# A fused attention and state-space kernel: x loaded in other runs, half of its transposes copied as 32-bit pairs, the first query projected into a score bank

## The chip, the cores and the metric

The kernel runs on one core of a Trainium2 chip. The metric is device time in microseconds (us) of one execution, the median of several. A profiled execution gives a trace; its span runs from the first to the last instruction, and a little time lies around it. The engines are TensorE (PE, its weight loads PEld), VectorE (DVE), ScalarE (ACT), GpSimd (POOL) and SyncE (SP, which issues most of the transfers).

## The reference, cut to what matters

Two branches read the same x (2048 tokens of 448 bfloat16 numbers) and are mixed by a gate:

```python
x = A_x
g = _sigmoid((x * gate_w).sum(-1, keepdims=True))
a = _A_ref(x, A_wq, A_wk, A_wv, A_wo)
b = _B_ref(x, B_A_re, B_A_im, B_B_re, B_B_im, B_C_re, B_C_im, B_log_dt, B_Dskip)
return g * a + (1 - g) * b
```

Branch A is attention with 16 query heads of 28 and one shared key and value head:

```python
q = (x @ wq).reshape(B, S, H, Dh).transpose(0, 2, 1, 3)
k = x @ wk
v = x @ wv
scores = jnp.einsum("bhqd,bkd->bhqk", q, k) * (Dh ** -0.5)
p = _softmax(scores, axis=-1)
o = jnp.einsum("bhqk,bkd->bhqd", p, v)
return o.transpose(0, 2, 1, 3).reshape(B, S, H * Dh) @ wo
```

Branch B is a long convolution of each channel of x with a kernel K that is built from 256 complex modes: K is the real part of the sum over n of C * exp(dt * A * l) * dt * B, for l from 0 to 2047.

## The kernel before, in words

**The long part.** The 16 x 16 x 4 score tiles (128 keys x 512 queries each) go through ACT's exponential at L1428 in sets of three and two tiles in turn. The scores come from TensorE into the five banks 0 to 4 of PSUM (`psS`), tile t in bank t % 5; bank 6 (`psB`) gathers the product with v; banks 5 and 7 are a pool of two that all other work borrows one after the other (`grp()`, with `lock` and `unlock`). Sets 0 to 5 take the query from `qT` (L1373), later ones from `qM` (L1396), a spread copy of `qT` that four transfers of POOL's queue make (L915). Beside the exponentials, VectorE builds tables for K, and TensorE makes K and the convolution.

**The start**, which the change touches. `loads` issues the transfers on SP's queue in the order x0, x1, x2, `raw0` (A_im, for branch B), x3, wq, wv with gate_w, `raw1` (A_re) and further ones; log_dt and wk go by ACT's queue. A block q of x is 512 tokens: partition p gets tokens 4p to 4p+3 of it, one run of 3584 bytes. `prep_x` then does, for q = 0 to 3:

- 16 transposes on TensorE (L668), eight for each half hp, into banks 2 * (q % 2) + hp;
- a copy of each half (112 x 1024) out of PSUM, which also puts the tokens, that lie 4 apart, in order: by VectorE (L680) for hp 1 of blocks 0, 1, 2, by ACT (L678) for the other five;
- the k projection (L688) into bank 4 (block 3: a bank of the pool) and its eviction by ACT to `kT` (L701); block q + 1 must wait for that of block q;
- `km`, the largest |k|, on VectorE (L696), and the v projection (L709).

From the four `km` VectorE makes `Wb` (L718, L720, L723): a matrix that gives each query its own bound, to be subtracted in the scores. The last step is `self.wbl`. The first query (`qproj(0)`): four matmuls with Wq (L893) into a bank of the pool, their absolute values on VectorE (L899), a matmul with `Wb` on top (L902), and the copy to `qT` (L905), for which the first scores wait. Wq is the wq transfer, spread by a copy of VectorE (L581).

At the same time `prep_params` starts branch B. `raw0`, transposed (L817), becomes a phase on VectorE (L828, L831, L832) and two sines on ACT (L834, L835). `raw1`, transposed, becomes t0 on VectorE (L828 again, through the helper `vt`, made at L839), from which ACT makes six exponentials: L840, and five of L843. A load of ACT's table stands between sines and exponentials. At L854 a further operation of VectorE is held back until `wbl` by an entry in `pg.after`.

**What sets the order.** Nothing runs in the order of the source. `Prog.schedule` plans all operations ahead with assumed times (the number that each `pg.op` is given, a model for transfers, fixed delays from engine to engine) and writes each engine's queue. At each step it takes, over all engines, the operation with the smallest (start, `pr`, index): what can start first goes first, and `pr` decides only among operations that could start at the same time, a lower one first. `pg.after[i] = j` keeps i from being planned before j. The chip then runs each queue in that order, whatever the real times are.

Of the kernel before, what the change touches and what calls it, by code (L numbers as in the profile page):

```python
# [7 lines left out]
ALU = mybir.AluOpType  # L8
AF = mybir.ActivationFunctionType
AX = mybir.AxisListType  # L10
BF = mybir.dt.bfloat16
F32 = mybir.dt.float32
P = 128

S = 2048
D = 448
# [3 lines left out]
DT = 112  # L20
# [20 lines left out]
XQ = NT * 512  # L41
QS = 4 * D + 64
GATE = (30, 35)
XDVE = ((1, 0), (1, 1), (1, 2))
WARM = 64
HELD = ((27, 3), (27, 9), (27, 15), (27, 21))
ROWS = 400
# [37 lines left out]
def dram(t, off, dims):  # L85
    return bass.AP(tensor=t.tensor, offset=t.offset + off, ap=[list(d) for d in dims])
# [326 lines left out]
def el(n, rate=0.96, fix=68):  # L413
    return fix + n / rate
# [14 lines left out]
class Kernel:  # L429
# [117 lines left out]
    def loads(self):  # L547
        pg, ins = self.pg, self.ins
# [1 line left out]
        x = ins["A_x"]  # L550

        def lx(q):
            pg.dma([(self.xst.v(0, P, q * QS, [[1, 4 * D]]), dram(x, q * 4 * P * D, [[4 * D, P], [1, 4 * D]]))],
                   (128, 3584), f"x{q}", wr=[("xst", q)], fac=0.85)
        self.raw = self.T
        self.late = []
        raw = self.raw
# [95 lines left out]
    def prep_x(self):  # L653
        pg = self.pg
        xst, kT = self.xst, self.kT
        sm = self.small
        for i in range(18):
            pg.op("pe", lambda e: e.matmul(self.psS.v(0, P, 4 * 512, [[1, 256]]), self.cst.v(0, P, 512, [[1, P]]), self.cst.v(0, P, 512, [[1, 256]]),
                                           start=True, stop=True, tile_position=(0, 0)), 213, rd=[("cst", 1)], wr=["warm", ("b", 4)], pr=3)
        for q in range(4):  # L660
            for hp in range(2):
                b = 2 * (q % 2) + hp
                t, o = self.bank(b, True)

                def mm(e, q=q, hp=hp, t=t, o=o):
                    for Tl in range(2):
                        for k in range(4):
                            r = e.matmul(t.v(0, P, o + 512 * Tl + 128 * k, [[1, 128]]),  # L668
                                         xst.v(0, P, q * QS + k * D + 2 * hp + Tl, [[4, P]]),
                                         self.ident.v(0, P, 0, [[1, P]]), is_transpose=True, tile_position=(0, 0))  # L670
                    return r
                pg.op("pe", mm, 600, rd=[("xst", q), "xpad", "id"], wr=[("b", b)])
                xT, xo = self.xq(q)
                dst = xT.v(0, DT, xo + 2 * hp * 512, [[512, 2], [4, 128], [1, 4]])
                src = t.v(0, DT, o, [[512, 2], [1, 128], [128, 4]])
                key = ("xT", hp, q)
                if (hp, q) not in XDVE:
                    pg.op("act", lambda e, d=dst, s=src: e.activation(d, s, AF.Copy), 1000, rd=[("b", b)], wr=[key])  # L678
                else:
                    pg.op("dve", lambda e, d=dst, s=src: e.tensor_copy(d, s), 1130, rd=[("b", b)], wr=[key])  # L680
            G = self.grp() if q == 3 else None
            t, o = self.bank(4)
            pk = (lambda G=G: G.v(0, P, 0, [[1, 512]])) if q == 3 else (lambda t=t, o=o: t.v(0, P, o, [[1, 512]]))
            bk = ("kx", 3) if q == 3 else ("b", 4)

            def mk(e, q=q, pk=pk, xT=xT, xo=xo):
                for T in range(NT):
                    r = e.matmul(pk(), self.Wk.v(0, DT, T * P, [[1, P]]),  # L688
                                 xT.v(0, DT, xo + T * 512, [[1, 512]]),
                                 start=(T == 0), stop=(T == 3), tile_position=(0, 0))  # L690
                return r
            o = pg.op("pe", mk, 1100, rd=["Wk"] + self.xk(q), wr=[bk], lock=G)
# [3 lines left out]
            km = lambda q=q, src=src: pg.op("dve", lambda e: e.tensor_reduce(  # L696
                sm.v(0, P, 8 + q, [[1, 1]]), src(), AX.X, ALU.max, apply_absolute_value=True), 600,
                rd=[bk if q == 3 else ("kT", q)], wr=[("km", q)])
            if q == 3:
                km()  # L700
            pg.op("act", lambda e, kv=kv, pk=pk: e.activation(kv, pk(), AF.Identity, bias=sm.v(0, P, 0, [[1, 1]])), 600,  # L701
                  rd=[bk, "s0"] + ([("km", 3)] if q == 3 else []), wr=[("kT", q)], pr=-2, unlock=G)
            if q < 3:
                km()

            for kt in range(4 * q, 4 * q + 4):
                def mv(e, kt=kt, xT=xT, xo=xo):
                    for T in range(NT):
                        r = e.matmul(self.psB.v(0, P, 32 * kt, [[1, 29]]), xT.v(0, DT, xo + T * 512 + 128 * (kt % 4), [[1, 128]]),  # L709
                                     self.Wv.v(0, DT, T * 32, [[1, 29]]), start=(T == 0), stop=(T == 3), tile_position=(0, 0))  # L710
                    return r
                pg.op("pe", mv, 140, rd=["Wv", "Wvg"] + self.xk(q), wr=[("b", 6)], pr=0.5)
            if q:
                o = pg.dma([(dram(self.XS, (q - 1) * DT * XQ, [[XQ, DT], [1, XQ]]), xT.v(0, DT, xo, [[1, XQ]]))],
                       (112, 4096), f"xs{q}", rd=self.xk(q), wr=[("XS", q)], pr=0.15)
                for i in self.late:
                    pg.after[i] = o.i
# [67 lines left out]
    def prep_params(self):  # L785
# [50 lines left out]
        pg.op("act", lambda e: e.activation(self.small.v(0, P, 3, [[1, 1]]), self.small.v(0, P, 2, [[1, 1]]), AF.Exp), 1340,  # L836
              rd=["dum", K(2), K(3)], wr=["dum2"], pr=-0.9)
        p1, k1 = trans(1, 1)
        vt(tt(0), p1, dtb, ALU.mult, [k1, "dt"], [K(0)], 1, unlock=p1)  # L839
        pg.op("act", lambda e: e.activation(t(5), t(0), AF.Exp), 950, rd=[K(0)], wr=[K(5)], pr=-1)  # L840
        for lv in range(5):
            ap9 = self.mq.v(0, P, lv * W2, [[32, 2], [64, NC], [1, 32]])
# [40 lines left out]
    def qproj(self, i):  # L883
        pg = self.pg
        qc, g = i // 4, i % 4
        s = i % 2
        X = ("qx", i)
        G = self.grp()
        px = lambda: G.v(0, P, 0, [[1, 512]])

        pr = 0.2 if i == 0 else 1.45 if i < 4 else 1.5
        for T in range(NT):
            pg.op("pe", lambda e, T=T: e.matmul(  # L893
                px(), self.Wq.v(0, DT, T * 512 + g * 128, [[1, 128]]),
                self.xT.v(0, DT, T * 512, [[1, 512]]), start=(T == 0), stop=(T == 3),
                tile_position=(0, 0), skip_group_check=True), 226,
                rd=["Wq"] + self.xk(0) + (["kap"] if i == 1 else []), wr=[X, ("q", s)], pr=pr, lock=G if T == 0 else None)
        av = self.qT.v(0, P, 512 * s, [[1, 512]])
        pg.op("dve", lambda e: e.tensor_reduce(  # L899
            av, G.v(0, P, 0, [[1, 512], [1, 1]]), AX.X, ALU.max, apply_absolute_value=True), el(512),  # L900
            rd=[X], wr=[("q", s)], pr=pr)
# [3 lines left out]
        o = pg.op("dve", lambda e: e.tensor_copy(self.qT.v(0, P, 512 * s, [[1, 512]]), px()), el(512),  # L905
                  rd=[X], wr=[("q", s)], pr=pr, unlock=G)
        if i == 0:
            self.qc0 = o.i
        if i in (3, 7, 11):
# [639 lines left out]
```

## Time and profile before

| | us |
|---|---|
| Median of three runs (497.34 to 498.5) | 497.38 |
| The profiled execution | 497.66 |
| Its span | 495.9 |
| PE busy | 461.8 |
| VectorE busy | 458.3 |
| ACT busy | 483.8 |
| POOL busy | 183.7 |
| First copy of x on ACT starts (L678) | 7.14 |
| First exponential of the scores starts (L1428) | 21.39 |

The granted clock of TensorE is 1.0 throughout. In the profile a line of the timeline gives the start, the duration, the engine, the line of the kernel, the operation, what it writes and reads with shapes, and in brackets how long its engine had been idle and what ended that. A line with "x2" is two such operations, whose durations are merged. A duration of VectorE or ACT overlaps the next one's start a little; where work is added up, the step from one start to the next is the better measure.

### The profile page before, as it was taken

What the parts mean: (1) busy time and instruction counts of PE and PEld (TensorE: products, weight loads), DVE (VectorE), ACT (ScalarE), POOL (GpSimd) and SP (SyncE); (2) the same over time, 40 slices, a digit from 0 to 9 for tenths busy, and PEclk for the clock granted to TensorE, in tenths of its full rate; (3) what the DMA queues carried; (4) which work ended last, traced back from release to release, by engine and by line L of the source; (5) the groups of instructions that cost most, each with busy time, mean ns of one, the idle gap of its engine ahead of it and who ended that gap; (6) DMA issues with size and microseconds to landing.
All of it is one profiled execution on the core that took longest, in us unless ns stands there. A gap on an engine that the chain in (4) does not pass through costs nothing.

```text
span 495.9 us, 17277 instructions
## 1 busy us (share of the span) xinstructions
PE 461.8 (93%) x7559; PEld 208.2 (42%) x7645; DVE 458.3 (92%) x872; ACT 483.8 (98%) x436; POOL 183.7 (37%) x331
## 2 busy tenths in 40 slices
PE   8899999999999999989989999999999999999997
PEld 6432233353443444444334344444534344444544
DVE  6999999999999999999999999999999999995324
ACT  6999999999999999999999999999999999999995
POOL 2102034234242528247707452643843525142110
PEclk9999999999999999999999999999999999999999
DMA  8997694927618554866943962698494685976752
GB/s 234 333 222 164 125 155 108 269 89 227 176 33 283 158 164 127 252 201 138 290 108 68 273 191 65 197 232 228 121 292 124 189 272 134 265 216 223 217 176 71
DMA packets 110055, 91.86 MB, mean 185 GB/s; under 512 B 35386, under 2 KB 105068, under 8 KB 109980
## 3 DMA queue, kind: packets, MB, share of 16 engines
q1 hardware_dynamic: 99322, 78.91, 57.9%
q0 software_dynamic: 10384, 11.70, 9.9%
q8 instruction: 60, 0.98, 0.8%
q10 hardware_dynamic: 274, 0.14, 0.1%
q14 instruction: 15, 0.12, 0.1%
HBM read 73.61 MB, written 5.23 MB: 159 GB/s over the span
## 4 chain that ended last, share of the span: by engine, by line
ACT 87%; PE 5%; DMA 2%; SPq 0%; issue 0%
ACT expT L1428 87%; DMA T<-KP_scratch 2%; PE psS L1373 1%; PE psS L1396 1%; PE psB L1349 1%; PE psB L1449 0%; PE psS L1286 0%; SPq L164 0%; PE psS L1047 0%; PE psS L893 0%; PE psB L1355 0%; PE psX L1047 0%; PE psS L776 0%; PE psX L1114 0%; PE psX L1135 0%
## 5 line engine op out<-in xcount | busy, mean ns | idle before, releaser
L1428 ACT ACTIVATE expT<-psS 128x1536 bf16<-128x1536 f32 (+1 forms) x410 | 464.2, 1407 | 1.1 <-PE psS L1396 0.4
L988 DVE TENSOR_TENSOR tab<-tab,mbf 128x512 bf16<-128x512 bf16 (+4 forms) x140 | 139.3, 998 | 0.0
L1373 PE MATMUL psS<-qT,kT 29*128 29x512 bf16 x684 | 95.7, 385 | 12.2 <-ACT expT L1428 7.1
L1449 PE MATMUL psB<-expT,vaug 128*32 128x512 bf16 x1000 | 99.9, 390 | 0.3
L1396 PE MATMUL psS<-qM,kT 128*128 128x512 bf16 x240 | 78.0, 382 | 13.1 <-issue 8.3
L164 POOL DMA_DIRECT2D KP_scratch<-kstg x104 | 57.3, 558 | 65.6 <-DVE kstg L1059 60.0
L1003 DVE TENSOR_TENSOR tab<-tab 128x256 bf16<-128x256 bf16 (+4 forms) x140 | 77.0, 570 | 0.0
L1449 PEld LDWEIGHTS psB<-expT,vaug 128*32 128x32 bf16 x1000 | 25.6, 93 | 72.6 <-issue 70.7
L164 POOL DMA_DIRECT2D qM<-qT x64 | 32.7, 518 | 58.1 <-DVE qT L905 37.5
L164 POOL DMA_DIRECT2D U<-T x49 | 36.7, 753 | 37.7 <-DMA U<-T 16.3
L1373 PEld LDWEIGHTS psS<-qT,kT 29*128 29x128 bf16 x684 | 23.7, 91 | 63.9 <-ACT expT L1428 51.3
L1355 PE MATMUL psB<-ident,one 128*128 128x512 bf16 x149 | 48.4, 384 | 0.0
L164 POOL DMA_DIRECT2D rdenB<-R_scratch x60 | 31.3, 527 | 32.4 <-DMA R_scratch<-denT 31.6
L1114 PE MATMUL psS<-T,U 128*26 128x128 bf16 (+3 forms) x1856 | 42.7, 221 | 0.4 <-issue 0.3
L1114 PEld LDWEIGHTS psS<-T,U 128*26 128x26 bf16 (+3 forms) x1856 | 32.9, 105 | 16.4 <-issue 11.4
L1017 DVE TENSOR_TENSOR tab<-tab,tmp 128x1984 bf16<-128x1984 bf16 x28 | 32.5, 1186 | 0.1
L1114 PE MATMUL psX<-T,U 128*32 128x128 bf16 (+3 forms) x1408 | 31.7, 221 | 0.4 <-DMA T<-KP_scratch 0.4
L1396 PEld LDWEIGHTS psS<-qM,kT 128*128 128x128 bf16 x316 | 18.9, 97 | 29.4 <-ACT expT L1428 20.0
L164 POOL DMA_DIRECT2D denT<-acc x15 | 10.8, 717 | 54.4 <-DVE acc L1173 54.4
L1114 PEld LDWEIGHTS psX<-T,U 128*32 128x32 bf16 (+3 forms) x1408 | 24.2, 105 | 11.6 <-issue 7.4
L1011 DVE TENSOR_TENSOR tmp<-tmp,mq 128x64 bf16<-128x64 bf16 (+4 forms) x70 | 25.3, 361 | 0.0
L934 DVE TENSOR_TENSOR msq<-seedz 128x512 f32<-128x512 f32 (+1 forms) x40 | 24.6, 615 | 0.0
(188 smaller groups left out, 503.7 us busy)
## 6 DMA issues: line engine op xcount, KB each, us to landing
T<-KP_scratch SPq DMA_DIRECT2D x204, 272.0 KB, 5.1
U<-KP_scratch SPq DMA_DIRECT2D x20, 272.0 KB, 5.7
rdenB<-R_scratch POOLq DMA_DIRECT2D x60, 64.0 KB, 3.8
U<-cst SPq DMA_DIRECT2D x1, 3584.0 KB, 23.6
qM<-qT POOLq DMA_DIRECT2D x64, 32.0 KB, 3.8
tab<-in_A_x_dram SPq DMA_DIRECT2D x4, 448.0 KB, 5.4
O<-in_A_x_dram SPq DMA_DIRECT2D x16, 112.0 KB, 8.2
O<-cst SPq DMA_DIRECT2D x1, 1792.0 KB, 8.5
```

Source lines behind the costliest of these rows:

```text
L164: return [e.dma_start(o, i, **kw) for o, i in pairs]
L934: pg.op("dve", lambda e: e.tensor_tensor(m2(msq), z2, z2, ALU.mult), el(2 * n), rd=[kr, ki] + first, wr=["msq"], pr=pr)
L988: mul = lambda e, o, a, b: e.tensor_tensor(o, a, b, ALU.mult)
L1003: vo(lambda e, dv=dv, tv=tv, k=k: e.tensor_tensor(dv, dv, tv, ALU.add if k else ALU.subtract), n, [kt[k], kd[k]], [kd[k]], 1.92 if lv else ...
L1011: vo(lambda e, w=w, lv=lv: e.tensor_tensor(rho.v(0, P, (32 - 2 * w) * 2, [[64, 32], [2, w], [1, 2]]), rho.v(0, P, (32 - w) * 2, [[64, 32], ...
L1017: vo(lambda e, k=k: e.tensor_tensor(tab.v(0, P, FM + k * FP + 2, [[64, 32], [2, 31], [1, 2]]), tab.v(0, P, lm + k * PL + 62, [[64, 32], [- ...
L1114: r = e.matmul(ps.v(32 * j, 32 - m0, 128 * k, [[1, 128]]), self.U.v(0, P, (4 * gi + j) % UA // 2 * 128 + 2 * (2 * m0 + par) + j % 2, [[4, ...
L1355: return e.matmul(t.v(0, P, off, [[1, 512]]), self.one.v(0, P, 2, [[0, P]]), self.ident.v(0, P, 0, [[0, 4], [1, P]]), start=b != 6, stop=b ...
L1373: r = e.matmul(self.psS.v(0, P, 512 * b, [[1, 512]]), kT.v(32 * h, DH + 1, 128 * kt, [[1, 128]]), qT.v(32 * h, DH + 1, 512 * (i % 2), [[1, ...
L1396: return e.matmul(self.psS.v(0, P, 512 * b, [[1, 512]]), kT.v(0, P, 128 * kt, [[1, 128]]), self.qM.v(0, P, (i % 2) * XQ + 512 * h, [[1, 51 ...
L1428: o = pg.op("act", lambda e: e.activation(expT.v(0, P, 512 * es[0], spread(es, n)), self.psS.v(0, P, 512 * bs[0], spread(bs, n)), AF.Exp, ...
L1449: r = e.matmul(self.psB.v(32 * h, 32, 0, [[1, 512]]), vaug.v(0, P, 32 * kt, [[1, 32]]), expT.v(0, P, 512 * ring[t], [[1, 512]]), start=(kt ...
```

## The change

- **Loads.** Partition p now gets tokens p, 128 + p, 256 + p and 384 + p of a block: four runs of 896 bytes in place of one of 3584. The planner's entry is adapted (512 runs of 896, factor 1.1).
- **Copies.** After the transposes the tokens of a half lie in order in PSUM, so the copy is of 1024 consecutive elements. VectorE has hp 1 of all four blocks now, as 512 elements of 32 bits; ACT has hp 0 of all four.
- **First query.** `qproj(0)` uses bank 4, one of the score banks, in place of a bank of the pool; it must wait for the eviction of the third k projection, and the second set of scores for it.
- **Order.** Transposes, copies and k projections get pr -0.3, -0.4, -0.5 and -0.6 by block (all were 0), `km` 0.05 for blocks 0 to 2 and -0.6 for block 3; t0 (L839) is held back until `wbl`; 16 warm-up matmuls (L658) in place of 18.

The diff, cut to its core:

```diff
-XDVE = ((1, 0), (1, 1), (1, 2))
+XDVE = ((1,0),(1,1),(1,2),(1,3))
+XPR = (-.3,-.4,-.5,-.6)
...
-            pg.dma([(self.xst.v(0, P, q * QS, [[1, 4 * D]]), dram(x, q * 4 * P * D, [[4 * D, P], [1, 4 * D]]))],
-                   (128, 3584), f"x{q}", wr=[("xst", q)], fac=0.85)
+            pg.dma([(self.xst.v(0, P, q * QS, [[D, 4], [1, D]]), dram(x, q * 4 * P * D, [[D, P], [P * D, 4], [1, D]]))],
+                   (512, 896), f"x{q}", wr=[("xst", q)], fac=1.1)
...
-        for i in range(18):
+        for i in range(16):
...
-                pg.op("pe", mm, 600, rd=[("xst", q), "xpad", "id"], wr=[("b", b)])
+                pg.op("pe", mm, 600, rd=[("xst", q), "xpad", "id"], wr=[("b", b)], pr=XPR[q])
                 xT, xo = self.xq(q)
-                dst = xT.v(0, DT, xo + 2 * hp * 512, [[512, 2], [4, 128], [1, 4]])
-                src = t.v(0, DT, o, [[512, 2], [1, 128], [128, 4]])
+                if (hp, q) in XDVE:
+                    dst = xT.cast(U32).v(0, DT, xo // 2 + hp * 512, [[1, 512]])
+                    src = t.cast(U32).v(0, DT, o // 2, [[1, 512]])
+                else:
+                    dst = xT.v(0, DT, xo + hp * 1024, [[1, 1024]])
+                    src = t.v(0, DT, o, [[1, 1024]])
...
-                    pg.op("act", lambda e, d=dst, s=src: e.activation(d, s, AF.Copy), 1000, rd=[("b", b)], wr=[key])
+                    pg.op("act", lambda e, d=dst, s=src: e.activation(d, s, AF.Copy), 1000, rd=[("b", b)], wr=[key], pr=XPR[q])
                 else:
-                    pg.op("dve", lambda e, d=dst, s=src: e.tensor_copy(d, s), 1130, rd=[("b", b)], wr=[key])
+                    pg.op("dve", lambda e, d=dst, s=src: e.tensor_copy(d, s), 630, rd=[("b", b)], wr=[key], pr=XPR[q])
...
-            o = pg.op("pe", mk, 1100, rd=["Wk"] + self.xk(q), wr=[bk], lock=G)
+            o = pg.op("pe", mk, 1100, rd=["Wk"] + self.xk(q), wr=[bk], lock=G, pr=XPR[q])
...
-                rd=[bk if q == 3 else ("kT", q)], wr=[("km", q)])
+                rd=[bk if q == 3 else ("kT", q)], wr=[("km", q)], pr=0.05 if q < 3 else XPR[q])
...
-        vt(tt(0), p1, dtb, ALU.mult, [k1, "dt"], [K(0)], 1, unlock=p1)
+        pg.after[vt(tt(0), p1, dtb, ALU.mult, [k1, "dt"], [K(0)], 1, unlock=p1).i] = self.wbl
...
-        G = self.grp()
-        px = lambda: G.v(0, P, 0, [[1, 512]])
+        if i == 0:
+            t_, o_ = self.bank(4)
+            G = None
+            px = lambda: t_.v(0, P, o_, [[1, 512]])
+        else:
+            G = self.grp()
+            px = lambda: G.v(0, P, 0, [[1, 512]])
+        bk = [("b", 4)] if i == 0 else []
```

The rest of it hands `bk` to the operations of `qproj`, so that bank 4 is kept for them.

More of the change, by code (lines that the diff above doesn't have):

```diff
@@ L12 @@
 F32 = mybir.dt.float32
+U32 = mybir.dt.uint32
 P = 128
@@ L896, in qproj @@
                 tile_position=(0, 0), skip_group_check=True), 226,
-                rd=["Wq"] + self.xk(0) + (["kap"] if i == 1 else []), wr=[X, ("q", s)], pr=pr, lock=G if T == 0 else None)
+                rd=["Wq"] + self.xk(0) + (["kap"] if i == 1 else []), wr=[X, ("q", s)] + (bk if T == 0 else []), pr=pr, lock=G if T == 0 else None)
         av = self.qT.v(0, P, 512 * s, [[1, 512]])
         pg.op("dve", lambda e: e.tensor_reduce(
-            av, G.v(0, P, 0, [[1, 512], [1, 1]]), AX.X, ALU.max, apply_absolute_value=True), el(512),
+            av, (G or Sub(self.bank(4)[0], self.bank(4)[1])).v(0, P, 0, [[1, 512], [1, 1]]), AX.X, ALU.max, apply_absolute_value=True), el(512),
             rd=[X], wr=[("q", s)], pr=pr)
@@ L905, in qproj @@
         o = pg.op("dve", lambda e: e.tensor_copy(self.qT.v(0, P, 512 * s, [[1, 512]]), px()), el(512),
-                  rd=[X], wr=[("q", s)], pr=pr, unlock=G)
+                  rd=[X] + bk, wr=[("q", s)], pr=pr, unlock=G)
         if i == 0:
```

## The prediction

> **What bounds the kernel now.** The first view is the page's busy time, the second its costliest groups.
>
> ```profile
> PE 461.8 (93%) x7559; PEld 208.2 (42%) x7645; DVE 458.3 (92%) x872; ACT 483.8 (98%) x436; POOL 183.7 (37%) x331
> ...
> L1428 ACT ACTIVATE expT<-psS 128x1536 bf16<-128x1536 f32 (+1 forms) x410 | 464.2, 1407 | 1.1 <-PE psS L1396 0.4
> ```
>
> ACT is busy for 483.8 of 495.9 us, and 464.2 of these are the softmax exponentials, before which it idles 1.1 us in all. The chain of work that ended last is 87% this line. So a change in the first 20 us counts only by what it does to ACT: the work it takes from ACT or gives it, and the idle time it opens or closes there. ACT's timeline of the start (start, duration, engine, line):
>
> ```profile
> 7.14 1.01 ACT L678 ACTIVATE xT<-psS 112x1024 bf16<-112x1024 bf16 x1
> ...
> 11.99 1.94 ACT L678 ACTIVATE expT<-psS 112x1024 bf16<-112x1024 bf16 x2 [0.21 <-PE psS L668]
> 14.51 0.95 ACT L834 ACTIVATE T<-T 128x896 f32<-128x896 f32 x1 [0.58 <-DVE T L832]
> ...
> 16.89 1.28 ACT L840 ACT_TABLE_LOAD   x1
> 18.19 0.95 ACT L840 ACTIVATE tab<-T 128x896 f32<-128x896 f32 x1
> 19.05 0.67 ACT L701 ACTIVATE kT<-psS,small 128x512 bf16<-128x512 f32 x1
> ...
> 19.71 1.78 ACT L843 ACTIVATE mq<-T 128x896 bf16<-128x896 f32 x2
> 21.39 1.44 ACT L1428 ACTIVATE expT<-psS 128x1536 bf16<-128x1536 f32 x1
> ...
> 31.41 2.37 ACT L1428 ACTIVATE expT<-psS 128x1536 bf16<-128x1536 f32 x2 [0.29 <-PE psS L1396]
> 33.93 6.20 ACT L1428 ACTIVATE expT<-psS 128x1536 bf16<-128x1536 f32 x5 [0.16 <-PE psS L1396]
> ```
>
> From 7.14 to the first exponential at 21.39 ACT idles only 0.22 + 0.22 + 0.21 + 0.58 = 1.23 us. It stays busy because L840 and two of the five L843, which all read t0 (written by VectorE at 15.69), fill 18.19 to 21.39 while the query is still being made. VectorE's timeline beside it:
>
> ```profile
> 10.00 0.69 DVE L696 TENSOR_REDUCE small<-kT 128x1 f32<-128x512 bf16 x1 [0.80 <-ACT kT L701]
> 10.60 1.08 DVE L828 TENSOR_TENSOR T<-psS,rdenB 128x896 f32<-128x896 bf16 x1
> ...
> 12.26 1.22 DVE L680 COPY expT<-psS 112x1024 bf16<-112x1024 bf16 x1
> 13.40 1.08 DVE L832 SCALAR_TENSOR_TENSOR T<-T 128x896 f32<-128x896 f32 x1
> ...
> 15.69 1.08 DVE L828 TENSOR_TENSOR T<-psX,cst 128x896 f32<-128x896 bf16 x1
> ...
> 18.82 0.35 DVE L723 SCALAR_TENSOR_TENSOR Wb<-expT,small,Wb 128x128 bf16<-128x128 bf16 x1
> 19.17 1.09 DVE L828 TENSOR_TENSOR seedz<-tab,T 128x896 f32<-128x896 f32 x1
> 20.18 0.68 DVE L905 CAST qT<-psX 128x512 bf16<-128x512 f32 x1
> ```
>
> From 10.00 on no gap is left on it: until Wb is ready (end of 18.82) VectorE, not ACT, sets the time of the first query. It cannot begin earlier: at 10.00 it waits for the first kT, that for ACT's copy at 7.14, and that for the table load before it, none of which the change touches.
>
> **The change, part by part.**
>
> *Copies on ACT.* Five of eight become four. One copy is worth its start-to-start step, 1.94/2 = **-0.97 us of ACT work**.
>
> *Copies on VectorE.* Three of 1.22 become four of 512 pairs each. The trace has no such copy. Below it stands the L831 row (896 f32 in 0.63, so 0.36 for 512), above it today's 1.22; nearest is L905, 512 words of 4 bytes out of PSUM in 0.68, and the int32 copy at L627 (896 in 0.93, one word a cycle) agrees. I take a step of 0.60, the distance from L905 to its follower (20.18 to 20.78). But the first two copies lie before 10.00, where VectorE idles anyway. Inside the full stretch one old copy (step 1.14) goes and two new ones come (1.20): **+0.06**. The ends are -0.5 and +1.2.
>
> *t0 behind Wb.* The L828 at 15.69 (step 1.01) leaves the stretch before Wb. The wait costs nothing by itself, but behind t0 on VectorE stands L905, and for t0 wait L840 and all five L843 on ACT.
>
> *New order.* The planner takes, over all engines, the operation with the earliest start, then the lowest pr. Followed with its own numbers (for the order alone), this rule reproduces the old order shown above; with the new pr it gives for VectorE from 10.00: km0, third pair copy, L828, L831, Wq copy, fourth pair copy, L832, km1, km3, km2, L899, L718, L720 with the two Wv copies around it, L723, then t0, then L905. TensorE does both transposes of the third block before L817 and the k projection, and the fourth block's before the third k projection.
>
> *Sum on VectorE*, in steps from the trace: 0.60 + 0.60 + 1.12 + 0.54 + 0.54 + 0.60 + 1.00 + 4 x 0.60 + 0.06 + 0.16 + 0.27 + 0.35 = 8.24, with about 0.15 for the first waits: Wb at 18.4, not 19.17. t0 then runs to 19.5, L905 follows at 19.5 instead of 20.18 (t0 holds it, as L828 at 19.17 holds it today), and the first exponential could start at 19.5 + 1.21 = 20.7.
>
> *ACT in this order.* It has less to do, but more to wait for: kT1 is 0.35 later (its projection stands behind L817), the sines start behind L832 at about 15.2 instead of 14.51, and when the table load is over (about 18.9) nothing is left until t0: L840 starts at 19.6 and ends a step of 0.86 later, at 20.47, with all five L843 ahead. Today ACT stands there, with five L843 to do, at 19.71. So ACT is **0.76 us behind**: the copy's 0.97 is spent, and 1.73 of idle time is added.
>
> *Given back later.* The exponentials at 31.41 and 33.93 wait 0.29 + 0.16 for TensorE, the first of them behind the qM transfer. The qM transfers start with L905, 0.7 earlier, and ACT comes 0.76 later: I count **-0.45**, by bounds -0.45 and 0.
>
> *x loads.* Four runs of 896 bytes replace one of 3584. Transfers by queue (packets, MB, share of 16 engines), between 2 and 3 us and between 40 and 44 us:
>
> ```profile
> q1 hardware_dynamic: 76, 0.27, 77.1%
> ```
>
> ```profile
> q1 hardware_dynamic: 1577, 1.26, 107.0%
> ```
>
> A 3584-byte packet took 0.771 x 16 us / 76 = 162 ns; one of 799 bytes on average 1.07 x 64 us / 1577 = 43.4 ns, so 896 bytes some 49 ns and four of them 195. With 8 rows an engine that is 0.26 us a load, 1.05 for four; between 8 and 9 us, with the queues full, the old packets were no faster (173 ns for 3.05 KB), which gives 0. The x landings themselves have room, but the wq transfer stands behind them: it was issued at 3.16 and landed 9.7 later, at 12.86, exactly when L831 ends in the new order, and the Wq copy then holds all of VectorE. So **0 to +1.05; I take +0.3**, as the engines were 77 and 91% busy in the first two microseconds and have room for a part.
>
> The Trainium skill speaks against this part too (DMA: Bandwidth & Descriptors, "How a descriptor splits into AXI transactions"): a run that doesn't start on a 256-byte boundary pays for the bytes before it. Every second run of 896 bytes starts so; by its beats and the per-packet overhead given beside it my estimate is some 15% more time for x, 0.8 us for four loads. The two rows above give 20% between them, so the trace agrees, as long as the queues aren't full.
>
> *First projection in bank 4, 16 warm-up matmuls.* With Wq copied by 13.6 and bank 4 free at 14.0, the projection runs behind the fourth k projection and its L899 isn't late; TensorE has cover there. Cost 0; if the bank were late, it would be by one ACT step, 0.57.
>
> **Sum.** The profiled execution took 497.66 (span 495.9 and 1.76 around it), 0.28 over the median 497.38. 497.66 + 0.76 - 0.45 + 0.3 = 498.27; on the median's scale **498.0**. This measurement can tell about 0.3%, 1.5 us, from no change; 0.6 is inside that.
>
> **Rivals.**
>
> *Slower: the wq transfer takes the place of the copies.* It decides from a landing after 12.86, microsecond for microsecond, as VectorE has no gap until Wb. Price at the bound: 1.05; if TensorE's two waits also stay, 497.38 + 0.76 + 1.05 = 499.2. For it: the wq load queues behind all x. Against it: full queues showed no difference. 0.25.
>
> *Faster: ACT keeps its cover.* If the order leaves the sines where they are and ACT finds work until t0, the copy counts in full: 497.38 - 0.97 - 0.45 = 496.0, and with half of the 1.23 of idle time gone, 495.4. For it: ACT's work up to the table load alone would end near 17.0. Against it: VectorE's full stretch, which became no shorter than t0 needs. 0.20.
>
> *The pairs are no faster.* Two copies of 1.22 in the full stretch: +1.2 over the forecast, 499.2. Against it: L627 and L905. 0.05.
>
> The forecast gets 0.50. The range reaches from the faster rival's 495.5 to 499.8, the slower ones with 0.6 for a later order that moves with the start. Faster by over 0.3% (below 495.9): 0.18, most of the faster rival; slower (above 498.9): 0.30, the two slower ones; within: 0.52.
>
> **What would show it.** Right: pair copies near 0.65; the t0 L828 directly behind L723 near 18.4; L905 near 19.5; a gap on ACT of 1 us or so before the first sine and of about 0.6 before L840; no wait near 31 and 34. Wrong: an idle VectorE before the Wq copy (the slower rival), exponentials before L840 or no gap before it (the faster one), or new waits of ACT for TensorE after 40 us, of which this sum has none.

## The result and the profile after

The changed kernel takes 500.25 us (median of 20 runs, 497.53 to 503.96) against 497.39 for the kernel before (20 runs, 496.86 to 498.5): ratio **1.0051** (95% interval 1.0038 to 1.0064). It is slower, by 2.5 us by this ratio and 2.9 between the medians, and it is unsteady: 11 of its 20 runs lie above 500.2, yet its fastest is about as fast as the median of the kernel before. The profiled execution took 499.69, span 497.7 (before: 497.66 and 495.9). Two profiled executions further down (the changed kernel again, and the change without the hold of t0) ran disturbed, at a granted clock of 0.98; their times are not compared.

Lines of the changed kernel are shifted: L686 is the copy of x on VectorE, L707 the eviction to kT, L729 the last step of Wb, L834 and L838 the parameter products, L846 and L849 the exponentials behind t0, L917 the query's copy, L1385 and L1408 the scores (from `qT` and from `qM`; not only sets 0 to 5 read `qT`, as was said above: from set 14 on the sets of three do again, so L1385 runs to the end), L1440 their exponential, L1126 the convolution, L1147 another small product, L1461 the product with v, L1071 the last cast of K.

Busy time and the costliest groups, after:

```profile
PE 461.3 (93%) x7558; PEld 207.6 (42%) x7642; DVE 458.1 (92%) x873; ACT 482.8 (97%) x435; POOL 182.4 (37%) x331
...
L1440 ACT ACTIVATE expT<-psS 128x1536 bf16<-128x1536 f32 (+1 forms) x410 | 464.3, 1419 | 2.2 <-PE psS L1385 1.5
...
L1126 PE MATMUL psS<-T,U 128*26 128x128 bf16 (+3 forms) x1792 | 41.4, 221 | 1.9 <-issue 1.8
```

ACT has 1.0 us less work (482.8, not 483.8), as the change promises. But the exponentials now wait 2.2 us for TensorE, where they waited 1.1, and TensorE itself stood still for 1.8 us before convolution matmuls for "issue": time in which it waited for nothing that the profile shows.

The start, VectorE and then ACT:

```profile
12.31 0.63 DVE L837 TENSOR_SCALAR T<-T 128x896 f32<-128x896 f32 x1
12.85 0.62 DVE L583 COPY Wq<-mbf 112x1792 bf16<-112x1792 bf16 x1
13.38 0.69 DVE L686 COPY expT<-psS 112x512 uint32<-112x512 uint32 x1
13.98 1.08 DVE L838 SCALAR_TENSOR_TENSOR T<-T 128x896 f32<-128x896 f32 x1
...
17.84 0.35 DVE L729 SCALAR_TENSOR_TENSOR Wb<-expT,small,Wb 128x128 bf16<-128x128 bf16 x1
18.11 1.08 DVE L834 TENSOR_TENSOR T<-psS,cst 128x896 f32<-128x896 bf16 x1
19.11 0.68 DVE L917 CAST qT<-psS 128x512 bf16<-128x512 f32 x1
```

```profile
15.10 0.95 ACT L840 ACTIVATE T<-T 128x896 f32<-128x896 f32 x1 [1.17 <-DVE T L838]
...
19.23 0.95 ACT L846 ACTIVATE tab<-T 128x896 f32<-128x896 f32 x1 [0.24 <-DVE T L834]
...
33.87 2.37 ACT L1440 ACTIVATE expT<-psS 128x1536 bf16<-128x1536 f32 x2 [0.16 <-PE psS L1408]
36.47 29.59 ACT L1440 ACTIVATE expT<-psS 128x1536 bf16<-128x1536 f32 x26 [0.23 <-PE psS L1408]
```

The pair copy steps 0.60 (13.38 to 13.98), Wq is there when it is wanted (no gap before 12.85), t0 stands behind Wb, and ACT waits 1.17 before the sines.

**Where the time went.** Number the 410 exponentials from 0 and subtract their starts, after less before. The tenth is 0.15 us later, the 60th 0.36 earlier, the 200th 0.54 earlier, the 370th (443 us) **0.65 earlier**. The 375th (450) is 0.14 later, the 396th 0.21 later, the 400th (479.5) **1.65 later**, the last 1.5. All of the loss of this execution comes after 443 us, in two steps. ACT after 440 us, before (one stretch without a wait) and after, then TensorE of the changed kernel around each wait:

```profile
439.42 49.71 ACT L1428 ACTIVATE expT<-psS 128x1536 bf16<-128x1536 f32 x44
```

```profile
450.00 26.00 ACT L1440 ACTIVATE expT<-psS 128x1024 bf16<-128x1024 f32 x23 [0.31 <-PE psS L1408]
477.26 13.24 ACT L1440 ACTIVATE expT<-psS 128x1536 bf16<-128x1536 f32 x12 [1.26 <-PE psS L1385]
```

```profile
448.40 0.39 PE L1408 MATMUL psS<-qM,kT 128*128 128x512 bf16 x1
449.90 0.45 PE L1147 MATMUL psX<-ident,cst 128*64 128x64 bf16 x16 [1.10 <-issue]
```

And the chain of waits:

```profile
474.83 1.31 issue
476.14 0.75 PE psS L1126 x40
476.89 0.35 PE psS L1385 x3
477.26 2.37 ACT expT L1440 x2
```

Both stops fall in mid-queue, with no semaphore ending them, and they lie 1019 recorded instructions apart: four times 256, but for the few records that a trace can lack. The seven traces of e9 to e15 (below) have some 85 more records of TensorE, and there the count comes out exactly: all eleven stops for issue of over 0.1 us after 40 us, at 178 to 479 us, begin at an instruction whose number leaves the same remainder divided by 256, to within one. The page's part on queues names what comes in pieces: `q8 instruction: 60, 0.98` (60 packets, MB), 16 KB each, one per 256 of TensorE's instructions. When a packet moves is seen in the transfers of narrow windows. After, 443.4 to 447.0 us and 447.0 to 448.1:

```profile
DMA packets 1092, 1.12 MB, mean 311 GB/s; under 512 B 80, under 2 KB 1074, under 8 KB 1092
q1 hardware_dynamic: 1055, 1.08, 95.0%
```

```profile
DMA packets 388, 0.42 MB, mean 380 GB/s; under 512 B 18, under 2 KB 387, under 8 KB 387
q1 hardware_dynamic: 387, 0.40, 101.8%
q8 instruction: 1, 0.02, 5.3%
```

In the first window the queues are full of table loads, and no block of instructions moves; it does in the second (447.24 to 448.17), and TensorE goes on 1.7 us after it has landed. What fills the queues is in SP's timeline, after and then before:

```profile
443.50 6.39 SPq L166 DMA_DIRECT2D U<-KP_scratch  x8
449.93 0.61 SPq L166 DMA_DIRECT2D out_dram<-O  x1
457.63 4.97 SPq L166 DMA_DIRECT2D KP_scratch<-kstg  x8
462.65 8.46 SPq L166 DMA_DIRECT2D T<-KP_scratch  x12
471.15 2.83 SPq L166 DMA_DIRECT2D U<-KP_scratch  x4
```

```profile
443.00 5.89 SPq L164 DMA_DIRECT2D U<-KP_scratch  x8
448.93 0.62 SPq L164 DMA_DIRECT2D out_dram<-O  x1
```

Each of these loads is 272 KB, the last tables of the convolution. If a block is asked for when TensorE enters the one ahead of it (256 instructions before the stop), the two late ones were asked for at 443.5 and 469.4 and moved 3.76 and 4.29 us later. (The expectations below count from 0.14 us later and say 443.3 and 469.3.) Before, the blocks asked for at 443.6, 467.0 and 472.9 moved 1.30, 3.47 and 3.04 us later, and TensorE reached their edges 3.0, 1.5 and 1.8 us after they had landed, without a stop. The kernel's planner knows the blocks and allows 4.8 us for one in this stretch (`BLOCK` and `FETCH`, in the constants of `Prog`); the two late ones took 6.4 and 6.75 from the request to the next instruction. The moment of the request is a reading, not a record: over all blocks of e9 to e15 the median block moves 0.6 to 1.1 us after TensorE has entered the one ahead, but a few move up to 1.7 us before, so some requests come earlier than this count has them.

### The profile page after: what moved, and what is told of

Same layout as the page of the kernel before. It is cut to its first block, busy times and chain, and to the rows that moved or that the text cites. A ratio compares the mean times of both kernels' runs of the same rounds, so it can differ in the third digit from the quotient of the medians.

```text
span 497.7 us, 17275 instructions
## 1 busy us (share of the span) xinstructions
PE 461.3 (93%) x7558; PEld 207.6 (42%) x7642; DVE 458.1 (92%) x873; ACT 482.8 (97%) x435; POOL 182.4 (37%) x331
## 4 chain that ended last, share of the span: by engine, by line
ACT 87%; PE 7%; issue 0%
ACT expT L1440 86%; PE psS L1408 1%; PE psX L1126 1%; PE psB L1461 1%; PE psS L1396 1%; PE psS L1385 1%; PE psS L1270 0%; PE psB L1455 0%; PE psB L1361 0%; PE psS L1126 0%; PE psS L1298 0%; PE psS L1245 0%; PE psX L905 0%; PE psS L1230 0%; PE psX L782 0%
## 5 line engine op out<-in xcount | busy, mean ns | idle before, releaser
L1440 ACT ACTIVATE expT<-psS 128x1536 bf16<-128x1536 f32 (+1 forms) x410 | 464.3, 1419 | 2.2 <-PE psS L1385 1.5
L1385 PE MATMUL psS<-qT,kT 29*128 29x512 bf16 x684 | 95.7, 385 | 14.0 <-ACT expT L1440 8.8
L1461 PE MATMUL psB<-expT,vaug 128*32 128x512 bf16 x1000 | 99.9, 390 | 0.0
L1408 PE MATMUL psS<-qM,kT 128*128 128x512 bf16 x242 | 78.4, 382 | 12.9 <-issue 8.8
L1461 PEld LDWEIGHTS psB<-expT,vaug 128*32 128x32 bf16 x1000 | 25.6, 93 | 73.2 <-issue 71.7
L1385 PEld LDWEIGHTS psS<-qT,kT 29*128 29x128 bf16 x684 | 23.7, 91 | 66.2 <-ACT expT L1440 54.6
L1126 PE MATMUL psS<-T,U 128*26 128x128 bf16 (+3 forms) x1792 | 41.4, 221 | 1.9 <-issue 1.8
L1126 PEld LDWEIGHTS psS<-T,U 128*26 128x26 bf16 (+3 forms) x1792 | 31.4, 105 | 16.4 <-issue 11.3
L1126 PE MATMUL psX<-T,U 128*32 128x128 bf16 (+3 forms) x1472 | 31.8, 221 | 0.0
L1408 PEld LDWEIGHTS psS<-qM,kT 128*128 128x128 bf16 x316 | 19.2, 97 | 27.0 <-ACT expT L1440 17.8
L1126 PEld LDWEIGHTS psX<-T,U 128*32 128x32 bf16 (+3 forms) x1472 | 24.6, 106 | 11.3 <-issue 8.5
L1059 PE MATMUL psX<-tab 128*64 128x128 bf16 x608 | 25.7, 223 | 0.0
```

Of the source, the lines that this page charges most:

```text
L1059: r = e.matmul(G.v(64 * u, 64, 128 * k, [[1, 128]]), tab.v(0, P, lo + comp * PL + cg * 64 + u, [[2, 64]]), tab.v(0, P, fo, [[64, 2], [mo - ...
L1126: r = e.matmul(ps.v(32 * j, 32 - m0, 128 * k, [[1, 128]]), self.U.v(0, P, (4 * gi + j) % UA // 2 * 128 + 2 * (2 * m0 + par) + j % 2, [[4, ...
L1385: r = e.matmul(self.psS.v(0, P, 512 * b, [[1, 512]]), kT.v(32 * h, DH + 1, 128 * kt, [[1, 128]]), qT.v(32 * h, DH + 1, 512 * (i % 2), [[1, ...
L1408: return e.matmul(self.psS.v(0, P, 512 * b, [[1, 512]]), kT.v(0, P, 128 * kt, [[1, 128]]), self.qM.v(0, P, (i % 2) * XQ + 512 * h, [[1, 51 ...
L1440: o = pg.op("act", lambda e: e.activation(expT.v(0, P, 512 * es[0], spread(es, n)), self.psS.v(0, P, 512 * bs[0], spread(bs, n)), AF.Exp, ...
L1461: r = e.matmul(self.psB.v(32 * h, 32, 0, [[1, 512]]), vaug.v(0, P, 32 * kt, [[1, 32]]), expT.v(0, P, 512 * ring[t], [[1, 512]]), start=(kt ...
```

## The experiments

Three theories. **A**: blocks of TensorE's instructions that are asked for while table loads fill the queues come late, at two edges in the last 50 us (an edge is where one block of 256 instructions ends and the next begins); the change only put the edges there. **B**: the new order itself makes the last K, and so the end, later (its last casts come at 456.91 and 459.68, before at 455.02 and 457.40). **C**: the start costs the time.

**The changed kernel again** (no edit).

> The changed kernel once more, nothing edited. Theory A (TensorE's instructions come in blocks of 256 by a transfer of 16 KB that is asked for when the block before is entered, and two of these land late behind the table transfers of the last 50 us): a median of 499 to 501 with runs 3 us and more apart, and in this trace again idle time of TensorE marked issue near 448 or 475, of a size other than 1.10 and 1.31. Theory B (the new order itself makes the last K later, and the end with it): the same gaps of ACT, as large as before. Theory C (the start is worse): ACT already late at 30 to 60 us.

Measured: 499.84 (11 runs), ratio 1.0034 (1.0015 to 1.0053); the kernel before took 498.04 there. The loss is no matter of one chip. (Each ratio here and below is to the kernel before on the same chip, which took 497.5 to 498.0.)

**Edges earlier by 64 and by 128 instructions, and the control.** The first 32 of the matmuls that add nothing (L1361, from 23 us on) are followed by one or two more, 32 columns wide, that the planner doesn't see, so no order changes:

```diff
         def warm(e):
-            return e.matmul(self.psB.v(0, P, 0, [[1, 512]]), ...)
+            r = e.matmul(self.psB.v(0, P, 0, [[1, 512]]), ...)
+            if not hasattr(e, "n") and self.extra > 0:
+                self.extra -= 1
+                for _ in range(1):
+                    r = e.matmul(self.psB.v(0, P, 0, [[1, 32]]), ...)
+            return r
```

> The changed kernel with 32 small matmuls between 23 and 85 us that add zeros, hidden from the planner: the order stays, every later edge between two blocks of 256 instructions comes 64 instructions earlier in the program. Theory A: the first late block is now asked for at 441.2, ahead of the eight transfers at 443.5, and is in time; the second is asked for at 467.7, among the table transfers, and may still be up to 1.6 late: 497.5 to 499.2, less than the unedited one. Theories B and C: no change from the unedited one, 499 to 501.

> As the shift by 64, with two small matmuls in each of the 32 places: edges 128 instructions earlier. Theory A: the two blocks are asked for at 440.2 and 465.6, when the queues are not yet full, and are needed at 445.7 and 471.3: no late block, 497.0 to 498.0 and runs within 1 us of each other. Theories B and C: no change, 499 to 501.

> The kernel before, with the same 64 small matmuls, so edges 128 instructions earlier. Theory A: a block is now asked for at 470.6, in the full queues, and needed at 474.7; with the 3 to 4 us that such loads waited in this stretch, the 1 us that one takes and 1.4 until TensorE goes on, it is 1.3 to 2 late: 498.4 to 499.4, runs further apart than the 1.6 us of before. Theories B and C: 497.4 within 0.4.

Measured: 498.73 (ratio 1.0022, 1.0008 to 1.0035), 498.67 (1.0024, 0.9997 to 1.0052) and, for the kernel before, 498.39 (1.0012, 0.9998 to 1.0025). Instructions that do nothing make the changed kernel some 1.1 us faster by the medians on this chip, though the intervals of the ratios overlap; neither B nor C has a reason for it. The stops show it more clearly than the times. With 64 no stop of over 0.2 us for issue is left after 440 us; with 128 one is (1.06, at 476.39), and the time misses A's 497.0 to 498.0. In the control one appears that the kernel before doesn't have (0.58, at 475.33), and its exponentials lose 0.73 us there; A had expected 1.3 to 2. But the shift from the start moves every edge of the program, and 0.7 to 1.0 us of the loss stayed.

**The last 32 table loads cut to an eighth of their bytes**, in both kernels; they leave out the rest, so the tables are stale and the convolution isn't computed.

```diff
-            to = bass.AP(..., ap=[[4 * rs, 32], [TC, 8], [1, TC]])
+            n = 1 if gi >= 48 else 8; to = bass.AP(..., ap=[[4 * rs, 32], [TC, n], [1, TC]])
```

> The last 32 table loads of the program (the T and U loads that SP issues between 438 and 474 us in the changed kernel) fetch one row in eight each; the tables they should fill are stale, so the output of the convolution is wrong. All queues of the engines are in the same order. Theory A (blocks of TensorE's instructions are fetched late because these loads fill the DMA queues): the block transfers asked for near 443 and 469 us start within about 1 us, TensorE's two idle stretches marked issue (1.10 and 1.31 us) are gone, ScalarE's waits of 0.3 and 1.3 us after 440 us are gone, and the lead over the kernel before that the changed kernel has at 443 us (0.65 us) is kept: time 496.5 to 497.6. Theory B (the order itself makes the last K later, 1.9 us): the last casts of K stay at 456.9 and 459.7 us and the loss of 1 us or more stays at the end: 498.5 to 500. Theory C (the start alone costs it): the first exponentials are unchanged and the loss stays: above 498.5.

> The kernel before with the same 32 table loads cut to one row in eight (the output of the convolution is wrong by that). Theory A: before had its blocks just in time, so little changes: 496.6 to 497.6, and the changed kernel with the same cut is 0 to 0.8 us faster than this one. Theory B: little changes here, and the changed kernel with the same cut stays 1 to 2 us slower than this one. Theory C: as B.

Measured: 497.77 and 497.87, ratios 0.9991 (0.9979 to 1.0003) and 0.9991 (0.9976 to 1.0006), both 0.2 to 0.3 us above A's ranges. The whole loss is gone, though the order is the same and the last casts of K are nearly as late as in the changed kernel (456.37 and 459.13). C falls. Against B alone this run isn't enough, as short loads would also bring late tables in sooner; but in the changed kernel itself TensorE waits for no table after 440 us, so a late K costs nothing there, and B falls too. ACT of the changed kernel with short loads after 440 us, and the window in which the block now moves (444.0 to 445.4):

```profile
438.92 49.67 ACT L1440 ACTIVATE expT<-psS 128x1536 bf16<-128x1536 f32 x44
```

```profile
q1 hardware_dynamic: 115, 0.09, 28.2%
q8 instruction: 1, 0.02, 5.8%
```

44 exponentials without a wait; and with the queues 28% busy the block moves 0.72 us after TensorE enters the one ahead. Of the next five, four move 0.1 to 1.2 us after TensorE's entry and one 0.5 before it by this count, which supports when a request is made. The lead over the kernel before is 0.65 us at 443 us and still 0.5 at the last exponential.

**Half of the cause.** The U tables issued from 443.5 us are loaded by 16 transfers of half the size, so that SP asks for the same bytes more slowly (16 issues took 11.35 us, the 8 whole ones 6.39); in a second kernel the first two T tables of the last four too. The third is the kernel before with the first split.

```diff
-        for h in range(4):
-            to = bass.AP(tensor=buf.h, offset=h * rs + o, ap=[[4 * rs, 32], [TC, 8], [1, TC]])
+        lst, m = [], 2 if gi in (50, 51) else 1
+        for h, j in [(h, j) for h in range(4) for j in range(m)]:
+            to = bass.AP(tensor=buf.h, offset=h * rs + o + j * 4 * TC, ap=[[4 * rs, 32], [TC, 8 // m], [1, TC]])
```

> The changed kernel with the two late U tables that SP issues from 443.5 us on loaded by 16 transfers of half the size instead of 8 (same bytes, same order on every engine). An issue on SP takes about 0.62 us whatever its size (the 8 writes of 16 KB: 4.97 us), so these bytes are asked for at about half the rate, over 10 us instead of 6.4. Theory A: the block of TensorE asked for at 443.3 us gets through in less than the 3.76 us it waited: start of its packet 1 to 2.5 us after the request, no idle time over 0.5 us marked issue near 449, the lead of 0.65 us over the kernel before is kept up to exponential number 390; the second stall (near 476) may stay or go, as it is up to 1.1 us earlier: 497.5 to 499.5 in all. Theory B (a late K by the order, or data of the tables coming late): the split tables land up to 4 us later, so no gain: 499.5 to 501.

> As the one before, and the first two of the four last T tables (from 462.7 us on) in half-size transfers too; the last two tables are then issued about 5 us later, near 474 to 479 us. Theory A: the block asked for near 469 us waits less than the 4.29 us of the changed kernel as well, both issue stalls are gone; in return the last tables land near 484 us, 2 to 5 us later, about when TensorE needs them, which may cost 0 to 3 us in the tail: 497 to 500.5. Theory B: 500 to 503.

> The kernel before with its two U tables (from 443 us on) in half-size transfers. Its blocks came just in time, so theory A expects no change in the lead of its exponentials: 497.0 to 498.3, ratio 0.998 to 1.001. Theory B expects the same or up to 1 us slower, as the tables land later.

Measured: 502.03 (1.0076, 1.0054 to 1.0098), 503.07 (1.0114, 1.0079 to 1.0149) and 498.62 (1.0015, 1.0003 to 1.0026). As times, the first two missed A's range: slower, not faster. As mechanism, the edges did what A said. In the first the block asked for at 444.2 moved 2.45 us later (not 3.76), and there is no stop near 449; but the block for the second edge, whose loads were not split, moved 4.74 us after its request and the stop (1.62 us, after one of 0.39 at 469.69) cost more than in the changed kernel (in this execution the granted clock was also halved behind it, from 478.1 to 481.5 us):

```profile
474.82 0.31 PE L1126 MATMUL psS<-T,U 128*28 128x128 bf16 x8
476.75 0.75 PE L1126 MATMUL psS<-T,U 128*26 128x128 bf16 x40 [1.62 <-issue]
```

In the second both requests were answered earlier (2.43 and 0.73 us), and no stop for issue is left. In its place TensorE waits for the tables, which now land 5 us later, and all that stands behind in its queue waits with it, the next scores too (ACT idles 5.12 us):

```profile
478.48 1.05 PE L1126 MATMUL psS<-T,U 128*32 128x128 bf16 x32 [4.73 <-DMA T<-KP_scratch]
```

So the loads can't just be slowed: then the tables are late. The third kernel, the one before with the split, lies 0.3 us above A's range (to 498.3).

**The late edges alone.** Nothing is moved before 389 us. From there on, 11 of TensorE's filler matmuls of 512 columns are cut into four of 128 (66 instructions more), or 9 of them into eight of 64 (126 more); the control is the kernel before with the first cut.

```diff
         def filler(e, b):
...
-            return e.matmul(t.v(0, P, off, [[1, 512]]), ...)
+            self.fi += 1
+            m = 4 if 138 <= self.fi <= 148 else 1
+            for j in range(m):
+                r = e.matmul(t.v(0, P, off + j * 512 // m, [[1, 512 // m]]), ...)
+            return r
```

> The changed kernel with 11 of TensorE's filler matmuls (those from 389 to 422 us, 512 columns of nothing added) each cut into four of 128 columns: 66 more instructions in TensorE's queue from there on, about the same busy time, the same order. Up to 389 us the kernel is the changed one, so all block edges before that are too. Theory A: the edges that stall in the changed kernel (asked for at 443.3 and 469.3 us) come 66 instructions earlier, where the shift of 64 from the start had requests answered in 0.9 and 1.2 us: no idle time over 0.6 us marked issue after 440 us, the lead over the kernel before stays 0.3 to 0.8 us to the last exponential: 496.7 to 498.0, ratio 0.998 to 1.001. If the rest that the shift from the start left (0.7 to 1.0 us over the kernel with short table loads) does not come from earlier edges but from the table loads themselves, it stays: 498.2 to 499. Theory B: no gain, 499.5 to 501.

> The same with 9 of these fillers each cut into eight of 64 columns: 126 more instructions. Theory A: as with the shift of 128 from the start one edge, then near 475 us, falls among the last table loads again and costs 0.5 to 1.2 us: 497.4 to 499, 0.3 to 1.2 us slower than the shift of 66. Theory B: 499.5 to 501.

> The kernel before with 11 fillers (from 389 us on) cut into four: 66 more instructions, the same order. Its edges had just enough room; A expects no stall or one of up to 0.8 us: 497.2 to 498.6, ratio 0.999 to 1.002. B expects no change.

Measured: 498.51 (1.0016, 0.9997 to 1.0036), **498.03** (1.0003, 0.9995 to 1.0012) and 498.49 (1.0010, 0.9980 to 1.0039); the kernel before 497.95. Moving only late edges takes nearly all of the loss away: the interval of the second lies clear of both of the unedited kernel's (1.0038 to 1.0064, and 1.0015 to 1.0053 on the other chip), with the last K again later than in the kernel before (458.83 against 457.40). The first misses A's range (to 498.0), and its interval alone decides nothing. Which shift is better came out the other way round than expected, and 0.5 us apart, within their intervals. The better one's profile still shows one stop (its scores have line L1413):

```profile
475.33 0.61 PE L1413 MATMUL psS<-qM,kT 128*128 128x512 bf16 x2
476.87 0.42 PE L1126 MATMUL psS<-T,U 128*28 128x128 bf16 x16 [0.93 <-issue]
```

It leads the kernel before by 0.81 us up to the 393rd exponential (469 us), and that stop takes the lead away: 0.12 late at the 400th.

**Parts of the change.** The loads and copies without the rest (old priorities, 18 warm-ups, pool bank, no hold); the change without the hold of t0; the change with the first query in a bank of the pool:

```diff
-        pg.after[vt(tt(0), p1, dtb, ALU.mult, [k1, "dt"], [K(0)], 1, unlock=p1).i] = self.wbl
+        vt(tt(0), p1, dtb, ALU.mult, [k1, "dt"], [K(0)], 1, unlock=p1)
```

```diff
-        if i == 0:
+        if False:
             t_, o_ = self.bank(4)
             G = None
```

> The kernel before with the loads in runs of 896 bytes and the pair copies on VectorE (all four blocks), but the old priorities, 18 warm-up matmuls, the first query in the pool and t0 not held. In its queues t0 stays ahead of Wb on VectorE and the L840 of ScalarE ahead of the fourth kT, as in the kernel before. Theory C (the start decides): ScalarE has 0.97 us less work and VectorE's stretch to Wb is about as long as in the kernel before, so the first exponential starts at 20.4 to 21.4 us and the exponentials after number 10 lead the kernel before by 0.3 to 0.9 us. Theory A: how much of that is left at the end depends on where the block edges of TensorE fall against the table loads, because the plan of the rest changes too: 496.5 to 500.5 in all, with the loss, if there is one, in idle time marked issue after 440 us. Theory B says the same of the time, but puts a loss into a later last K.

> The changed kernel with t0 no longer held back until Wb; all else as it is. In VectorE's queue t0 then stands just ahead of the last step of Wb, and another product takes its place ahead of the query's copy. Theory C: ScalarE gets L846 0.2 to 0.4 us earlier, while the query comes up to 1.0 us later (20.1 us), with work of ScalarE to cover it: first exponential at 21.2 to 21.9 us with one more L849 done before it, exponentials after number 10 within 0.5 us of the changed kernel's. Theory A: the end again depends on the block edges: 496.5 to 500.5, any loss over 0.5 us in idle time marked issue after 440 us.

> The changed kernel with the first query back in a bank of the pool; all else as it is. Theory C (the bank matters at the start): the query is borrowed a pool bank that the parameter transposes then have to wait for; VectorE's order to Wb is unchanged or t0 comes up to 1 us later; the first exponential at 20.9 to 22 us. Theory A: whatever the start gives, the end depends on the block edges, which come at other places because the order of TensorE changes: 496.5 to 501, with any loss over 0.5 us in idle time marked issue after 440 us or in TensorE's wait for the spread query near 33 us.

Measured: 508.82 (1.0212, 1.0188 to 1.0235), 498.90 (1.0020, 1.0003 to 1.0036) and 500.38 (1.0062, 1.0036 to 1.0088). The loads and copies alone are worst, by 10.8 us, far outside what any theory expected. With the old priorities the fourth k projection is planned late, VectorE stands idle for it, and the first exponential starts at 23.23:

```profile
19.59 0.69 DVE L701 TENSOR_REDUCE small<-psX 128x1 f32<-128x512 f32 x1 [1.50 <-PE psX L693]
```

That is 1.4 us at the tenth exponential; a part of it is the granted clock, which was halved from 18.3 to 21.8 us in this execution (the projection took 1.57 us, 1.04 in the changed kernel). Most of the rest is at the end: SP writes the last K at 468.18 (457.63 with the whole change), and the span goes on for 15 us behind the last exponential's end, before for 7. This looks like B's mechanism, by another plan; no run tests it. With the pool bank ACT waits 1.16 us for TensorE's scores near 32 us (0.16 with bank 4), and the tenth exponential is 0.97 late. But the granted clock was halved from 24.4 to 27.8 us in this execution, so how much of that is the bank's isn't shown. The rest of its loss lies at an edge once more: TensorE stops 1.39 us for issue at 178.28, and ACT waits 1.11 behind it. Without the hold, the query comes 0.5 us later (L917 at 19.63, behind one more product on VectorE), and ACT waits 1.88 and 0.48 us near 33 and 35 us. Here too the granted clock was halved, from 28.0 to 34.8 us, so these waits don't show what the hold is worth, and that the time is nonetheless nearer to the kernel before (1.0020) than the change's (1.0051) contradicts nothing.

## Why the prediction was wrong

498.0 was forecast, with 499.8 as the upper end and 0.30 for slower; it is 500.25.

**Right: the start's rows.** ACT bounds, and its one copy less is 1.0 us of its busy time. Pair copy: step 0.60, as taken, so the rival of pairs that are no faster falls. Order on VectorE: as derived, Wq copy and fourth pair copy included. Wb ready near 18.1 (forecast 18.4), L917 at 19.11 (19.5), first exponential at 20.92 (20.7), a wait of 1.17 before the sines ("1 us or so"). Bank 4 costs nothing that shows, as forecast; with the pool bank in its place (e12) the tenth exponential came 0.8 later, part of it by the halved clock.

**Start terms, too dark by about half a microsecond.** L846 started at 19.23, not 19.6, so ACT was 0.38 behind, not 0.76. The waits near 34 and 36 us stayed (0.16 + 0.23 against 0.29 + 0.16): -0.06, not -0.45. The x loads cost nothing that shows: first kT at 9.27 (9.28 before); x landed at 4.0 us least, 5.6 median and 7.9 at most from issue (3.5, 5.4 and 8.6 before), so the +0.3, the row-based bound of 1.05 and the rival of a late wq transfer all fall. The Trainium skill's price for runs that don't start aligned (DMA: Bandwidth & Descriptors, "How a descriptor splits into AXI transactions"), which I put at 0.8 us for the four loads, can't be read off these landings: the earliest is 0.5 later, the last 0.7 earlier. Summed, these terms gave +0.61; measured at the tenth exponential: +0.15 in the profiled executions, and from -0.32 to +0.15 in six others with the same start. Near 77 us the kernel before waits 0.26 for the product with v, which the changed one doesn't, so by 443 us the changed kernel leads. How far differs from one execution to the next: of those with the same start, some stop at an edge near 178 us (0.32 in e5, 0.69 in e9) and some don't. In e5 and e6, where no block is late after 440 us, the two kernels' times are equal: the start is worth about nothing in the median.

**The step that failed** is the last one named there: "new waits of ACT for TensorE after 40 us, of which this sum has none". There are two, 0.31 and 1.26 us, and the starts of the exponentials move by 0.8 and 1.45 us there, 2.2 in all. In the profiled execution that takes the lead of 0.65 away and leaves 1.5 at the last exponential, most of the 2.0 us that this execution took longer. The upper end had 0.6 us in reserve for "a later order that moves with the start"; that a new plan of the first 20 us also moves TensorE's instruction blocks and the table loads of the last 50 against each other was not thought of. The profile of before did show how near it was: the block asked for at 467.0 waited 3.47 us, and TensorE reached its edge 1.5 us after it had landed, about the time that TensorE takes to go on after a late one (1.2 to 1.7).

The likeliest case was "no change", and for the start alone it was right; the time came out slower by another mechanism than either slower rival's.

**Open.** The changed kernel's time scatters over 6 us, and the late blocks are not all of that. A granted clock of 0.996 to 0.997 shows in seven of its runs, all above 500.2 (median 502.0); the other thirteen have a median of 499.4, so some 2 us of the loss is there at the full clock. One stretch of 3.4 us at half the clock gives just such a mean (1.7 of 500 us), and the profiles of e7, e9, e10 and e12 show five such stretches before the last few us. Each begins within 1.4 us of the end of a stop of TensorE (0.6 to 4.7 us long), so there the stop came first. But the stops of 1.10 and 1.31 above were not followed by one, and the stretch in e8 from 28.0 us follows only stops of 0.6 us and less; what decides that, and which edges stop in which execution, no run tells. Of the kernels that do the whole computation none was faster than the kernel before; the best of the changed ones (e14) is level with it.

## What to carry to other kernels

In a long unrolled program an engine's instructions are traffic too: when the profile says "issue" in the middle of a busy queue, compare the time with the packets of the instruction queue and with what else fills the queues. Look at the granted clock of the same stretch before a wait is put down to an edit. A plan that is remade by a change in its first microseconds must be judged over the whole span: subtract the starts of the repeated operation, number by number, and the place of the loss shows by itself. Where such edges sit among bulk loads with little to spare, a handful of idle instructions more or less is worth as much as the change itself.

## What the runs showed of the hardware

- TensorE's instructions came in 16 KB packets, one per 256 instructions. With the last table loads cut short (the queues 28% busy in the window shown) a block moved 0.1 to 1.2 us after TensorE entered the one ahead; behind the whole loads (95% and more) it took up to 4.7 us, the packet about 1 us, and after a stop TensorE went on 1.2 to 1.7 us after its end.
- The Trainium skill says that crossing a block is "mostly hidden" (Runtime: NRT & Kernel Launch, "Instruction fetch mechanics"), with blocks of 256 instructions and the next one fetched while the current one runs. The size and the prefetch agree with these traces; hidden it is in most of the 60 blocks, but not while large loads fill the queues: 1.10 and 1.31 us here, up to 1.62 in another run.
- Halving the size of each load did slow the flow of bytes, nearly by half (16 issues in 11.35 us, 8 whole ones in 6.39), which brought the blocks in sooner and the tables later.
- The granted clock can halve for a few microseconds in an execution whose mean is 0.993 to 0.997: 3.4 us at a time in e7, e9, e10 and e12, each time within 1.4 us of the end of a stop of TensorE.
